# Keys and queries of the first batch in long pieces, turned by products with the identity

## The chip, the core and the metric

The kernel runs on one core of a Trainium2 chip. The metric is device time in microseconds (us) of one launch. The five engines are written as in the profile: PE (TensorE) with PEld (its weight loads), DVE (VectorE), ACT (ScalarE), POOL (GpSimd) and SP (SyncE, which here only issues DMAs). Each engine works through its own list in order and waits at the head of it.

## What is computed

Attention in chunks of 32 tokens, then two MLPs, all in f32:

```
q_c = q[:, :, c_start:c_end]                       # 32 queries
k_ctx, v_ctx = k, v[:, :, c_start-16 : c_end+8]    # cut at the ends of the sequence
scores = q_c @ concat(mem_k, k_ctx).T / 8          # 8 memory keys ahead of 56 others
out[:, :, c_start:c_end] = softmax(scores) @ concat(mem_v, v_ctx)
x = out as 3072 x 512
x = (s * relu(x @ w_in)**2 + b) @ w_out            # 512 -> 2048 -> 512
y = (silu(x @ w_gate) * (x @ w_val)) @ w_out2      # 512 -> 1536 -> 512
```

There are 4 batches of 8 heads, 768 tokens and a head width of 64.

## The kernel before

**Tiles.** Tokens go through attention in 24 groups g of 128 (six per batch, four chunks each), and through the first MLP in 8 blocks t of 384 tokens (three groups). The first MLP has 16 weight columns m of 128: `first_up(t, m)` (U in the lists) makes 12 products into `hp`, DVE and ACT square the result and split it into `ghi` and `glo`, and `first_down(t, m, i)` (D) adds 12 products to the four banks `acc0` to `acc3`. Each weight tile (1 MB, `load_w1`) is split by DVE and ACT into a rounded part and a rest, `w_first`, before it can be used: `split` makes the steps magnitude, bound, shift, sign, rest, hi, lo, of which five to seven are DVE's.

**The first batch.** Groups 0 to 5 (`EARLY`) are prepared in a way of their own. `load_tokens(g)` (K in `LOADS`) fetches keys and queries of one group by four to six DMAs, token by token: each piece of one head and one token is 64 numbers, 256 bytes. `stage_queries` and `stage_keys` turn them with PE's transpose (12 per group) into PSUM, and DVE or ACT copy them to `qt` and `kt`, where every chunk gets its window of 64 keys. Then come, per group, scores (S, `stage_scores`), maximum and shift on DVE, exponential on ACT, the turned probabilities (A, `stage_probs`), the product with the values (V, `stage_values`), normalising on DVE, and the turn into `xhi`, `xlo` (X, `stage_turn`, `stage_x`). Scores and values each take both banks of the pool `ps_a`, so one has to be emptied by DVE before the next may start. The values come through POOL's queue into one of two buffers (`load_values`, `g % 2`).

**Order.** All lists are made ahead by `Plan.run`, a list scheduler with a length for every step and counters for buffers (`rings`, `room`). `START` gives PE's order of the first blocks: the stages of groups 0 to 5 and, among them, five U and four D. `LOADS` chains the first issues on SP's queue; `MOVED` names the steps that go to the other one of DVE and ACT. `LENT` counts the weight slots (of 17) that the first batch borrows.

```
START = (
    "Q0 T0 S0 Q1 T1 A0 V0 Q2 S1 T2 X0 A1 S2 V1 Q3 A2 X1 V2 T3 X2 Q4 S3 U U D T4 D A3 V3 U Q5 "
    "S4 X3 T5 U A4 S5 D V4 A5 X4 V5 D X5 U "
)
```

The last U of `START` is the first of block t = 1; it needs X5. From there on PE has work in an unbroken row of U and D.

Of the kernel before, what the change touches and what calls it, by code (L numbers as in the profile page):

```python
# [10 lines left out]
F32 = mybir.dt.float32  # L11
# [17 lines left out]

START = (  # L30
    "Q0 T0 S0 Q1 T1 A0 V0 Q2 S1 T2 X0 A1 S2 V1 Q3 A2 X1 V2 T3 X2 Q4 S3 U U D T4 D A3 V3 U Q5 "
    "S4 X3 T5 U A4 S5 D V4 A5 X4 V5 D X5 U "
# [12 lines left out]
    "K0 C K1 W0 W1 K2 K3 W3 W7 W2 K4 W5 W8 K5 W4 W6 K6_0 W12 W10 W11 W9 W14 W13 W15 "  # L45
# [102 lines left out]
def attention_and_two_mlps(  # L148
# [53 lines left out]
    LENT = 3  # L202
    EARLY = 2 * GPB

# [10 lines left out]
    ident = const.tile([P, P], F32, name="ident")  # L215
    make_identity(nc, ident)
    sb = const.tile([P, 2], F32, name="sb")
# [78 lines left out]
    def rows(dst, src, b, heads, first, n):  # L296
# [6 lines left out]
    def load_tokens(g):  # L303

        b, gi = divmod(g, GB)
        s0 = gi * GQ
        t = wp.tile([P, 4, H * D], F32, tag="w", name=f"qk{g}")
        tq, ka, kb, sc = (t[:, i] for i in range(4))
        every = slice(0, H)
        a, z = s0 - LEFT, s0 + GQ + RIGHT  # L310
        left, over, n = max(0, -a), max(0, z - S), HALF - NMEM
        rows(ka, mem_k, b, every, 0, NMEM)
        if left:
            rows(ka[NMEM:], k, b, every, 0, left)
        rows(ka[NMEM + left:], k, b, every, a + left, n - left)
        rows(tq, q, b, every, s0, GQ)
        rows(kb, k, b, every, a + n, HALF - over)
        if over:
            rows(kb[HALF - over:], k, b, every, S - over, over)
        loaded.setdefault(g, {}).update(q=tq, ka=ka, kb=kb, sc=sc)  # L320
# [73 lines left out]
    def load_values(g, queue):  # L394
# [3 lines left out]
        n = g % 2  # L398
        if n not in v_bufs:
            v_bufs[n] = ld.tile([P, NC, NP, D + 1], F32, tag=f"v{n}", name=f"v{n}")  # L400
            nc.gpsimd.memset(v_bufs[n][:, :, :, D:], 1.0)
        tv = v_bufs[n]
        for e in range(2):
            p0 = e * KC
            if gi < 2:
                mem = tv[p0:p0 + NMEM]
                queue.dma_start(out=mem[:, 0, :, :D], in_=mem_v[b, e:H:2].rearrange("h s d -> s h d"))
# [1014 lines left out]
```

## Time and profile before

| what | value |
|---|---|
| three runs | 1214.85, 1216.21, 1216.58 us (median 1216.21) |
| the profiled execution: its own time, which is its span | 1216.5 us |
| mean granted TensorE clock | 0.987 of full |
| PE, PEld busy | 1175.4 us (97%), 1116.4 us (92%) |
| DVE, ACT busy | 751.7 us (62%), 502.7 us (41%) |
| POOL busy | 143.6 us (12%) |
| DMA | 175.60 MB, mean 144 GB/s |

A row of the timeline gives the start and the length of a run of equal instructions, its engine and line, what it writes and reads, and in brackets the idle time of its engine before it with what ended that. A table of windows gives each engine's busy time in a stretch; an engine that is idle there waits for another, or has nothing to do.

### The profile page before, as it was taken

The numbers are of one execution on the slowest core, as the hardware profiler recorded it, in microseconds if no ns is written. First come the engines' busy times: TensorE is split into PE (matmuls) and PEld (weight loads), VectorE is DVE, ScalarE is ACT, GpSimd is POOL, SyncE is SP. The second block draws the span as 40 slices with busy tenths as digits, with TensorE's granted clock in tenths as the row PEclk, the third lists the DMA queues.
The fourth block names the chain that finished last, engine by engine and source line by source line (L and its number), as shares of the span: only waits on it lengthen the run. The fifth ranks groups of instructions, "written<-read, shape, count | busy, mean of one in ns | idle before, by whom it ended". The sixth has DMA issues, their size and how long they took to land.

```text
span 1216.5 us, 23342 instructions
## 1 busy us (share of the span) xinstructions
PE 1175.4 (97%) x9220; PEld 1116.4 (92%) x9220; DVE 751.7 (62%) x1324; ACT 502.7 (41%) x865; POOL 143.6 (12%) x232
## 2 busy tenths in 40 slices
PE   5679999999999999999999999999999999999998
PEld 4568999999999999999999999999999999999997
DVE  5789986655555445544487955569853367743343
ACT  3365543233333434332277545446433234432332
POOL 6342013222132223120000000000000000000000
PEclk9689999999999999999999999999999999999999
DMA  9947334222222222220347266386555386465351
GB/s 193 240 115 208 114 94 110 66 45 65 40 53 68 44 66 47 46 55 1 113 182 251 104 235 218 121 318 259 188 229 216 123 331 246 152 247 208 108 204 52
DMA packets 171775, 175.60 MB, mean 144 GB/s; under 512 B 115170, under 2 KB 141090, under 8 KB 170642
## 3 DMA queue, kind: packets, MB, share of 16 engines
q1 hardware_dynamic: 164498, 162.92, 41.7%
q0 software_dynamic: 7168, 11.18, 4.0%
q8 instruction: 73, 1.20, 0.4%
q14 instruction: 36, 0.29, 0.1%
HBM read 125.24 MB, written 48.76 MB: 143 GB/s over the span
## 4 chain that ended last, share of the span: by engine, by line
PE 89%; SPq 7%; DMA 1%; DVE 1%; issue 1%; ACT 0%; DVEq 0%; ACTq 0%
PE acc L615 7%; PE hp L614 7%; PE acc L614 7%; PE acc L616 7%; PE hp L616 7%; PE hp L615 7%; PE chain_A L615 6%; PE chain_A L616 6%; PE oacc L616 6%; PE oacc L615 6%; PE chain_A L614 5%; PE oacc L614 5%; PE chain_B L614 4%; PE chain_B L615 4%; PE chain_B L616 4%; SPq L298 3%
## 5 line engine op out<-in xcount | busy, mean ns | idle before, releaser
L614 PE MATMUL hp<-xhi,w_first 128*128 128x384 f32 x512 | 174.7, 341 | 1.1 <-DVE xhi L232 1.1
L614 PE MATMUL acc<-ghi,w_first 128*128 128x384 f32 x512 | 173.3, 338 | 1.5 <-DVE ghi L667 0.9
L615 PE MATMUL acc<-glo,w_first 128*128 128x384 f32 x512 | 171.9, 336 | 0.9 <-DVE glo L674 0.5
L615 PE MATMUL hp<-xlo,w_first 128*128 128x384 f32 x512 | 172.2, 336 | 0.2 <-DVE xlo L609 0.2
L616 PE MATMUL hp<-xhi,w_first 128*128 128x384 f32 x512 | 172.1, 336 | 0.0
L616 PE MATMUL acc<-ghi,w_first 128*128 128x384 f32 x512 | 171.3, 335 | 0.0
L416 POOL DMA_DIRECT2D v<-in_v_dram x208 | 134.0, 651 | 312.5 <-PE psB L549 266.3
L784 ACT ACTIVATE kept<-chain_A 128x384 f32<-128x384 f32 x144 | 70.8, 492 | 186.0 <-PE chain_A L616 183.9
L615 PE MATMUL chain_A<-ops,hi_up 128*128 128x384 f32 x384 | 130.1, 339 | 0.0
L616 PE MATMUL chain_A<-ops,lo_up 128*128 128x384 f32 x384 | 129.4, 337 | 0.0
L614 PE MATMUL chain_A<-ops,hi_up 128*128 128x384 f32 x384 | 128.4, 334 | 0.0
L654 DVE SCALAR_TENSOR_TENSOR r<-r,sb 128x384 f32<-128x384 f32 x87 | 53.2, 612 | 112.9 <-ACT r L643 112.3
L643 ACT ACTIVATE r<-hp 128x384 f32<-128x384 f32 x98 | 48.0, 490 | 176.1 <-PE hp L616 159.1
L616 PE MATMUL oacc<-w_down,glo 128*128 128x512 f32 x288 | 114.6, 398 | 0.0
L615 PE MATMUL oacc<-w_down,ghi 128*128 128x512 f32 x288 | 113.9, 396 | 0.0
L614 PE MATMUL oacc<-w_down,ghi 128*128 128x512 f32 x288 | 112.1, 389 | 0.0
L614 PEld LDWEIGHTS hp<-xhi,w_first 128*128 128x128 f32 x512 | 96.9, 189 | 2.6 <-issue 1.4
L614 PEld LDWEIGHTS acc<-ghi,w_first 128*128 128x128 f32 x512 | 96.1, 188 | 3.3 <-ACT v L230 1.2
L615 PEld LDWEIGHTS acc<-glo,w_first 128*128 128x128 f32 x512 | 96.1, 188 | 2.7 <-DVE glo L674 1.6
L789 DVE TENSOR_TENSOR kept<-chain_B,kept 128x384 f32<-128x384 f32 x48 | 26.7, 557 | 114.5 <-PE chain_B L616 112.2
L615 PEld LDWEIGHTS hp<-xlo,w_first 128*128 128x128 f32 x512 | 96.9, 189 | 0.5 <-DVE xlo L609 0.5
L616 PEld LDWEIGHTS hp<-xhi,w_first 128*128 128x128 f32 x512 | 96.8, 189 | 0.0
(131 smaller groups left out, 2213.2 us busy)
## 6 DMA issues: line engine op xcount, KB each, us to landing
ops<-ops_dram SPq DMA_DIRECT2D x56, 768.0 KB
ops_dram<-ops SPq DMA_DIRECT2D x28, 768.0 KB
sum_dram<-o SPq DMA_DIRECT2D x48, 256.0 KB
v<-in_v_dram POOLq DMA_DIRECT2D x176, 56.0 KB, 3.4
raw_first<-in_moe_w_in_dram SPq DMA_DIRECT2D x16, 512.0 KB
raw_first<-in_moe_w_out_dram SPq DMA_DIRECT2D x16, 512.0 KB
o<-sum_dram SPq DMA_DIRECT2D x8, 1024.0 KB
y_dram<-y SPq DMA_DIRECT2D x32, 192.0 KB
```

Of the source, the lines that this page charges most:

```text
L298: nc.sync.dma_start(out=dst.rearrange("p (h d) -> p h d", d=D)[:n], in_=src[b, heads, first:first + n, :].rearrange("h s d -> s h d"),)
L416: queue.dma_start(out=tv[r0:r0 + n, c, :, :D], in_=v[b, e:H:2, first:first + n, :].rearrange("h s d -> s h d"),)
L614: nc.tensor.matmul(o, whi, xhi, start=first, stop=False, skip_group_check=onto)
L615: nc.tensor.matmul(o, whi, xlo, start=False, stop=False, skip_group_check=onto)
L616: nc.tensor.matmul(o, wlo, xhi, start=False, stop=last, skip_group_check=onto)
L643: nc.scalar.activation(out=r, in_=hp, func=AF.Relu)
L654: nc.vector.scalar_tensor_tensor(out=r, in0=r, scalar=s_sb, in1=r, op0=ALU.mult, op1=ALU.mult)
L784: nc.scalar.activation(out=t, in_=st2[n]["A"], func=AF.Copy)
L789: nc.vector.tensor_tensor(out=t, in0=st2[n]["B"], in1=kept, op=ALU.add)
```

## The change

Keys and queries of batch 0 no longer come group by group. Two DMAs fetch all keys (four heads each) and four fetch the queries (four heads and half of the partitions each): partition p gets tokens 6p to 6p+5 of a head in one run of 6 x 64 numbers, 1536 bytes. PE turns them for a whole block of 384 tokens at a time: for each pair of heads j and each of the six tokens r of a partition, `turn_pieces` multiplies the pieces (as the stationary side, 64 columns per head) with the identity, and writes the columns into PSUM six apart, which puts the tokens in order. For keys the identity is padded by three columns on either side, so that the window of block u is 69 partitions wide. One copy per pair of heads spreads keys to all twelve chunks of a block (`copy_batch_keys`), into the tiles of `xhi`, `xlo` for block 0 and over the fetched queries for block 1. Six weight slots are borrowed in place of three; values get a third early buffer in one of them. `START`, `LOADS` and `MOVED` are new; groups 1 and 3 (and 6 and 7) now take the exponential head by head on ACT with the maximum as bias, so DVE makes no shift for them. Groups 6 and later are loaded as before.

```diff
-    "Q0 T0 S0 Q1 T1 A0 V0 Q2 S1 T2 X0 A1 S2 V1 Q3 A2 X1 V2 T3 X2 Q4 S3 U U D T4 D A3 V3 U Q5 "
-    "S4 X3 T5 U A4 S5 D V4 A5 X4 V5 D X5 U "
+    "K0 Q0 S0 S2 A0 V0 X0 S1 A1 V1 A2 X1 V2 Q1 X2 K1 U S3 U D A3 S4 U V3 D A4 U X3 S5 D V4 A5 X4 "
+    "D V5 X5 U "
...
-    "K0 C K1 W0 W1 K2 K3 W3 W7 W2 K4 W5 W8 K5 W4 W6 K6_0 W12 W10 W11 W9 W14 W13 W15 "
+    "K6_0 BK0 C BM BK1 BQ00 BQ01 W0 BQ11 W1 BQ10 W2 W3 W6 W5 W4 W8 W7 W9 W12 W11 W10 W14 W13 W15 "
...
-    LENT = 3
     EARLY = 2 * GPB
+    LENT = 6
+    RES = GB * GQ // P
+    PAD = 3
+    EDGE = PAD * RES - LEFT
...
+    def VBUFS(g):
+        return 3 if g < EARLY else 2
...
+    def load_batch(name, src, i, half=None):
+        at = slice(0, P) if half is None else slice(half * (P // 2), (half + 1) * (P // 2))
         nc.sync.dma_start(
-            out=dst.rearrange("p (h d) -> p h d", d=D)[:n],
-            in_=src[b, heads, first:first + n, :].rearrange("h s d -> s h d"),
-        )
+            out=pieces(name)[at].rearrange("p h r d -> p h (r d)"),
+            in_=src[0, 4 * i:4 * i + 4].rearrange("h (p r) d -> p h (r d)", r=RES)[at],
+        )
...
+    def turn_pieces(name, j, ps, rows, turned):
+
+        n = turned.shape[1]
+        to = ps[:, 0:RES * n].rearrange("m (p r) -> m r p", r=RES)
+        for r in range(RES):
+            for e in range(2):
+                nc.tensor.matmul(
+                    to[e * D:(e + 1) * D, r], pieces(name)[rows, 2 * (j % 2) + e, r], turned, start=True, stop=True
+                )
+
+    def stage_batch_keys(u, j):
+        batch["k", u, j] = ps = bank(ps_acc, f"acc{j}", f"psK{u}_{j}")
+        span, first = P // 2 + 2 * PAD - 1, u * P // 2
+        turn_pieces(f"keys{j // 2}", j, ps, slice(0, P), padded[:, first:first + span])
...
+    def copy_batch_keys(engine, u, j):
+        w = batch.pop(("k", u, j))[:, EDGE:EDGE + 1]
+        copy(
+            engine, early_keys(u)[j // 2][:, j % 2, :, NMEM:],
+            bass.AP(tensor=w.tensor, offset=w.offset, ap=[w.ap[0], [CHUNK, GPB * NC], [1, WIN]]),
+        )
...
+    def stage_batch_queries(t, j):
+        pool, tag = (ps_acc, f"acc{j}") if t else ((ps_a, "a"), (ps_h, "h"))[j // 2]
+        batch["q", t, j] = ps = bank(pool, tag, f"psQ{t}_{j}")
+        at = slice(t * (P // 2), (t + 1) * (P // 2))
+        turn_pieces(f"queries{j // 2}", j, ps, at, ident[at, at])
...
-        n = g % 2
+        n = g % VBUFS(g)
```

**SP's queue at the start.** Before, the first ten DMAs (`qk` is a group's tile of keys and queries, `sb_in` two constants):

```order
L298 DMA qk_141<-in_mem_k_dram 8x8x64
L298 DMA qk_141<-in_k_dram 16x8x64
L298 DMA qk_141<-in_k_dram 56x8x64
L298 DMA qk_141<-in_q_dram 128x8x64
L298 DMA qk_141<-in_k_dram 80x8x64
L262 DMA sb_in<-in_moe_s_dram 1x1
L262 DMA sb_in<-in_moe_b_dram 1x1
L298 DMA qk_164<-in_mem_k_dram 8x8x64
L298 DMA qk_164<-in_k_dram 72x8x64
L298 DMA qk_164<-in_q_dram 128x8x64
```

Now, from the fourth DMA on (three small ones for group 6 stand ahead; `keys` and `queries` hold four heads of all 768 tokens, `raw_first` is a weight tile as fetched):

```order
L320 DMA keys_161<-in_k_dram 128x4x384
L270 DMA sb_in<-in_moe_s_dram 1x1
L270 DMA sb_in<-in_moe_b_dram 1x1
L326 DMA keys_161<-in_mem_k_dram 8x8x64
L320 DMA keys_167<-in_k_dram 128x4x384
L320 DMA queries_169<-in_q_dram 64x4x384
L320 DMA queries_207<-in_q_dram 64x4x384
L249 DMA raw_first_226<-in_moe_w_in_dram 128x4x256
L254 DMA raw_first_226<-in_moe_w_out_dram 128x1024
L320 DMA queries_207<-in_q_dram 64x4x384
```

The keys of all six groups and the queries of the first three now come ahead of the first weight tile; before, the keys and queries of two groups did, and those of the other four came between weight tiles.

**PE's list from its first work to the first scores (`psS`).** Before:

```order
L268 MATMUL spread<-ident,sb_in 128x1 x2
L434 MATMUL psQ_175<-ident,qk_141 128x128 x4
L445 MATMUL psK_0_181<-ident,qk_141 128x80 x4
L445 MATMUL psK_1_186<-ident,qk_141 128x80 x4
L481 MATMUL psS_0_213<-kt_205,qt_203 32x64
```

Now (each `psK`, `psQ` row is one turn for a pair of heads):

```order
L276 MATMUL spread<-ident,sb_in 128x1 x2
L377 MATMUL psM<-ident,keys_161 128x8 x4
L336 MATMUL psK_0_180<-ident,keys_161 64x69 x12
L336 MATMUL psK_1_209<-ident,keys_161 64x69 x12
L336 MATMUL psK_2_230<-ident,keys_167 64x69 x12
L336 MATMUL psK_3_245<-ident,keys_167 64x69 x12
L336 MATMUL psQ_0_259<-ident,queries_169 64x64 x12
L336 MATMUL psQ_1_273<-ident,queries_169 64x64 x12
L336 MATMUL psQ_2_288<-ident,queries_207 64x64 x12
L336 MATMUL psQ_3_303<-ident,queries_207 64x64 x12
L537 MATMUL psS_0_332<-early_khi,qt_286 32x64
```

Twelve transposes stood ahead of the first scores; now 96 products do, for three groups at once. The same eight turns for block 1 stand later, just ahead of the first U.

**DVE's list at the last early part of x (`xlo` of group 5).** Before:

```order
L586 TENSOR_TENSOR on_1225<-psV_1_1172,rc_1219 128x4x64
L955 TENSOR_TENSOR w_first_1210<-raw_first_877,w_first_1210 128x1024
L232 CAST xhi_950<-psO_1243 128x4x128
L609 TENSOR_TENSOR xlo_951<-psO_1243,xhi_950 128x4x128
L232 COPY y<-acc_770 128x384
L906 SCALAR_TENSOR_TENSOR raw_first_402<-raw_first_402,t_first_852 128x1024
L913 SCALAR_TENSOR_TENSOR raw_first_402<-raw_first_402 128x1024
```

Now:

```order
L958 TENSOR_SCALAR t_first_1117<-t_first_1117 128x1024
L963 SCALAR_TENSOR_TENSOR raw_first_598<-raw_first_598,t_first_1117 128x1024
L666 TENSOR_TENSOR xlo_1194<-psO_1354,xhi_1193 128x4x128
L1012 TENSOR_TENSOR w_first_1348<-raw_first_663,w_first_1348 128x1024
L970 SCALAR_TENSOR_TENSOR raw_first_598<-raw_first_598 128x1024
L443 STREAM_TRANSPOSE qt_143<-qt_143 128x512
L447 STREAM_TRANSPOSE kin_142<-kin_142 128x640
L451 COPY memT_1398<-kin_142 128x32
L950 TENSOR_SCALAR t_first_1405<-raw_first_1338 128x1024
```

Seven weight tiles were wholly split ahead of this place, and are five now; the sixth and most of the seventh follow it.

## Rows read from the trace of the kernel before

**Rows 1.** The page's 40 slices, 30.4 us each: busy tenths, granted clock, DMA.

```profile
PE   5679999999999999999999999999999999999998
PEclk9689999999999999999999999999999999999999
DMA  9947334222222222220347266386555386465351
```

**Rows 2.** Windows: per engine busy time (x instructions), then granted clock, DMA share, GB/s.

```profile
0.00:12.00 12.00, 4.61 (x81) 3.93 (x82) 2.18 (x6) 1.28 (x1) 9.72 (x23) 1.00 0.92 166
12.00:20.00 8.00, 4.93 (x80) 3.95 (x80) 4.89 (x15) 5.18 (x8) 5.33 (x9) 1.00 1.09 262
20.00:37.00 17.00, 8.33 (x216) 6.53 (x216) 16.42 (x30) 5.07 (x7) 7.21 (x12) 0.87 1.16 231
37.00:52.00 15.00, 7.39 (x152) 5.94 (x152) 7.40 (x15) 5.71 (x10) 9.00 (x13) 0.50 1.07 212
52.00:92.60 40.60, 32.48 (x482) 28.44 (x466) 35.63 (x63) 24.15 (x42) 13.99 (x22) 0.86 0.56 138
92.60:175.30 82.70, 81.35 (x640) 79.36 (x641) 78.54 (x120) 41.84 (x66) 11.77 (x19) 1.00 0.49 139
```

**Rows 3.** Timeline of PE, the front: start, length, what, idle before it.

```profile
8.95 1.27 PE L445 MATMUL psK<-ident,qk 80*128 80x80 f32 x8
10.61 1.34 PE L481 MATMUL psS<-kt,qt 64*32 64x64 f32 x64 [0.38 <-DVE kt L232]
...
24.67 1.09 PE L434 MATMUL psQ<-ident,qk 128*128 128x128 f32 x4 [6.42 <-DMA qk<-in_q_dram]
...
38.23 1.12 PE L534 MATMUL psA<-ident,qk 128*128 128x128 f32 x4 [2.40 <-ACT qk L514]
...
50.09 1.09 PE L434 MATMUL psQ<-ident,qk 128*128 128x128 f32 x4 [6.19 <-DMA qk<-in_q_dram]
51.11 1.19 PE L481 MATMUL psS<-kt,qt 64*32 64x64 f32 x64
52.23 0.69 PE L614 MATMUL hp<-xhi,w_first 128*128 128x384 f32 x1
...
92.59 0.41 PE L614 MATMUL hp<-xhi,w_first 128*128 128x384 f32 x1 [1.08 <-DVE xhi L232]
```

**Rows 4.** The chain of work that ended last, pieces in order of time: start, length, what.

```profile
13.44 6.93 SPq L298
...
37.25 7.45 SPq L298
```

**Rows 5.** DMA queue q1 from 19 to 26 us: packets, MB, share of 16 engines.

```profile
q1 hardware_dynamic: 2820, 0.82, 81.1%
```

**Rows 6.** The same queue from 103 to 115 us, where weight tiles land.

```profile
q1 hardware_dynamic: 4266, 3.86, 104.9%
```

**Rows 7.** Groups by form, DVE, 0 to 100 us: busy us, mean ns, idle before.

```profile
L913 DVE SCALAR_TENSOR_TENSOR raw_first<-raw_first 128x1024 uint32<-128x1024 uint32 x8 | 9.8, 1222 | 0.1
L955 DVE TENSOR_TENSOR w_first<-raw_first,w_first 128x1024 fp32r<-128x1024 f32 x7 | 8.5, 1218 | 0.2 <-ACT w_first L230 0.2
L901 DVE TENSOR_SCALAR t_first<-t_first 128x1024 uint32<-128x1024 uint32 x8 | 5.5, 692 | 0.2
L507 DVE TENSOR_TENSOR qk<-psS,mx 128x256 f32<-128x256 f32 x12 | 4.5, 415 | 0.0
L232 DVE COPY kt<-psK 128x448 f32<-128x448 f32 x4 | 2.5, 615 | 0.0
L232 DVE COPY qt<-psQ 128x512 f32<-128x512 f32 x3 | 2.1, 686 | 0.9 <-PE psQ L434 0.9
L232 DVE COPY kt<-psK 128x64 f32<-128x64 f32 x5 | 1.1, 221 | 4.8 <-ACT kt L230 4.8
```

**Rows 8.** Waits of 0 to 110 us: us in total, times, longest.

```profile
ACT t_first L891 <- DMA raw_first<-in_moe_w_out_dram: 14.1, 3, 7.2
```

**Rows 9.** Timeline of DVE: the last rest of a weight tile's split.

```profile
172.01 1.22 DVE L955 TENSOR_TENSOR w_first<-raw_first,w_first 128x1024 fp32r<-128x1024 f32 x1
```

More of the change, by code (lines that the diff above doesn't have):

```diff
@@ L294, in attention_and_two_mlps, with lent, pieces @@
     v_bufs = {}
-    def rows(dst, src, b, heads, first, n):
+    def VBUFS(g):
+        return 3 if g < EARLY else 2
+    batch = {}
+    def lent(name):
+        if name not in batch:
+            batch[name] = wp.tile([P, 4, 512], F32, tag="w", name=name)
+        return batch[name]
+    def pieces(name):
+        return lent(name)[:, 0:3].rearrange("p a f -> p (a f)").rearrange("p (h r d) -> p h r d", h=4, r=RES)
+    def load_batch(name, src, i, half=None):
+        at = slice(0, P) if half is None else slice(half * (P // 2), (half + 1) * (P // 2))
@@ L997, in plan_queries @@
             return
-        qk = transfer(
-            [], lambda: load_tokens(g), 4, 590, take=["sc"], rate=200.0, name=f"K{g}"
-        )
-        vv = load_v(g)
-        at_[g] = {"v": vv, "qk": qk}
-        t = plan.add(PE, 0.44, lambda: stage_queries(g, early), [qk], take=["acc2"] if early else ["a"])
-        at_[g]["qt"] = either(
-            f"q{g}", {ACT: 0.50, DVE: 0.60}, lambda e: stage_queries_copy(e, g), [t], take=["qt"],
-            give=["acc2"] if early else ["a"],
-        )
@@ new lines, in attention_and_two_mlps, with plan_batch, load @@
+    early_ready = {}
+    def plan_batch():
+        def load(name, src, i, half, of):
+            batch_landed[name] = transfer(
+                [], lambda: load_batch(of, src, i, half), 1, 786 if half is None else 393, rate=BATCH_RATE, name=name
+            )
+        for i in range(2):
+            load(f"BK{i}", k, i, None, f"keys{i}")
+        batch_landed["BM"] = transfer([issues["BK0"]], load_memory, 1, 16, rate=40.0, name="BM")
+        for t in range(2):
+            for i in range(2):
+                load(f"BQ{t}{i}", q, i, t, f"queries{i}")
+        for g in range(VBUFS(0)):
+            at_[g] = {"v": load_v(g)}
@@ new lines, in plan_batch_keys @@
+    def plan_batch_keys(u):
+        done = []
+        if u == 0:
+            t = plan.add(PE, 0.30, stage_memory, [batch_landed["BM"]], take=["h"])
+            batch_landed["m"] = plan.add(DVE, 0.12, copy_memory_keys, [t], give=["h"])
+        for j in range(NP):
+            t = plan.add(
+                PE, 0.78, lambda j=j: stage_batch_keys(u, j), [batch_landed[f"BK{j // 2}"]], take=[f"acc{j}"],
+                put=["w"] * 2 if u and j == NP - 1 else (),
+            )
+            done.append(either(
+                f"k{u}_{j}", {ACT: 0.75, DVE: 0.85}, lambda e, j=j: copy_batch_keys(e, u, j),
+                [t, *(early_ready["q", 1, "pe"] if u else ())],
+                take=["x"] if not u and j == 0 else (), give=[f"acc{j}"],
+            ))
+        for i in range(2):
+            done.append(either(
+                f"m{u}_{i}", {ACT: 0.40, DVE: 0.30}, lambda e, i=i: fill_batch_memory(e, u, i),
+                [batch_landed["m"], *(done[:1] if not u else early_ready["q", 1, "pe"])],
+            ))
+        early_ready["k", u] = done
@@ new lines, in plan_batch_queries @@
+    def plan_batch_queries(t):
+        done, pe = [], []
+        for j in range(NP):
+            ring = [f"acc{j}"] if t else [("a", "h")[j // 2]]
+            p = plan.add(
+                PE, 0.66, lambda j=j: stage_batch_queries(t, j), [batch_landed[f"BQ{t}{j // 2}"]], take=ring,
+            )
+            pe.append(p)
+            done.append(either(
+                f"q{t}_{j}", {ACT: 0.43, DVE: 0.47}, lambda e, j=j: copy_batch_queries(e, t, j), [p],
+                take=() if t else ["r"], give=ring,
+            ))
+        early_ready["q", t], early_ready["q", t, "pe"] = done, pe
```

197 lines of the change are left out of this document (103 added, 94 removed), and 23 rows, old and new, of the table MOVED.

## The prediction

> **What bounds the kernel now.** I read the page's slices first [rows 1]: PE is full from the fourth slice to the end, at full clock. So the time is what PE does from about 92 us on, which the change leaves alone, plus the moment at which that unbroken row begins. Call T0 the start of the fifth U, the first of block t = 1: 92.6 us [rows 3]. The windows say what the front is made of [rows 2]. Up to 52 us the 16 DMA engines are at 0.92 to 1.16 of their time; from 52 to 92.6 us they are at 0.56, and DVE is busy 35.6 of 40.6 us. So two limits follow each other: data until 52 us, then DVE. Added up, DVE works 2.2 + 4.9 + 16.4 + 7.4 + 35.6 = 66.5 us before T0 and idles 26.1.
>
> The timeline of PE shows the data limit twice, 6.4 and 6.2 us of waiting for a group's queries [rows 3]; ACT waits 14.1 us for weight tiles [rows 8], and the chain of waits runs through single token loads that hold SP's queue for 7 us [rows 4]. Between 37 and 52 us DVE is idle for 7.6 of 15 us [rows 2].
>
> The clock: the slices read nearly full in the first one [rows 1], but the row of four transposes at 38.2 us, inside a stretch granted 0.50 [rows 2, 3], lasts 1.12 us, and the like row at 24.7 us lasts 1.09. So I price the front at the lower level, 1.2 GHz, until PE has worked without a gap for some time.
>
> **What the change does, part by part.**
>
> *Loads.* Keys and queries of six groups are 3.46 MB in 256-byte pieces (six groups of 256 KB of queries, 304 KB of keys, 16 KB of memory keys). While such pieces fill the queue it moves 0.82 MB in 81.1% of 7 us, 144 GB/s [rows 5]; a mix of weight tiles and small loads of group 6 moves 3.86 MB in 12.6 us of engine time, 307 GB/s [rows 6]. The change needs 3.16 MB. At 307 that is 10.3 us of the DMA engines instead of 24.0; the ends are 144 (a gain of 2) and 307, and I take 260, 12 us, as 1536-byte pieces are nearer to those of a weight tile. So weight tiles land some 12 us earlier, and the waits for queries at 24.7 and 50.1 us and most of ACT's 14.1 us go. SP's held issues go with them. Two tiles fewer are fetched ahead, so their loads compete later; from 92.6 us on the DMA engines are at 0.49 [rows 2], which hides them, and without that cover one tile costs 1 MB at 307, 3.4 us.
>
> *A later start.* Before, the scores of group 0 ran at 10.6 us. Now all keys and half of the queries, 2.4 MB, with about 0.5 MB of values beside them, must land before the first score, at 166 to 262 GB/s [rows 2] some 12 to 16 us after about 1 us of start-up. PE turns as they land.
>
> *Turns.* Eight turns of twelve products stand ahead of the first score, eight more ahead of the first U. No row has such a product. The 32 score products leave 64 rows in 1.19 to 1.34 us [rows 3]: an f32 product counts twice, a transpose once. The 24 of a turn cost 24 x 0.019 = 0.45 us at the scores' rate. But scores fill eight blocks of the array at a time and a turn two: twelve follow each other in a block instead of eight, each with 69/64 of the columns, and 1.19/8 x 12 x 69/64 = 1.9 us. The far end is one after another at the pace of the 80-column transposes, 24 x 1.27/8 = 3.8 us. I take 1.4, below 1.9 because the scores' 1.19 holds a start and an end that turns in a row pay once, and 0.9 at full clock. First turn at about 8.7 us, when PE's first work before ended too (8.95); eight take 11.2, scores at 20, DVE's first maximum at 21.5 instead of 12.1. **This part costs some 9 us of start.**
>
> A transpose is a mode of its own, and the Trainium skill, "TensorEngine Tiling (Array Packing)", Restrictions, says that column tiling (64 columns here) excludes transpose mode for f32; "TensorE: Matmul & The Clock Gate", Terms, calls that mode four times faster for f32. By it half the batch's queries, three transposes of 1.09 us, would cost 13 us as products, 6.5 in two blocks, 1.6 per turn; the doubled rows agree in kind, and the sum would be 3 us worse.
>
> *DVE's work ahead of T0.* Moved behind T0: one rest (1.22), two lo steps (2.44), five steps of 0.69 (3.46) [rows 7], 7.1 us. Copies of keys and queries: three of 0.686, four of 0.615, five of 0.221 go, 5.6 us; two of 672 columns (0.615 x 1.5) and four smaller, 3.6, come. The shifts of groups 1 and 3 go, 4 x 0.415, for two tiny steps; the rest evens out. Sum 66.5 - 7.1 - 2.0 - 1.4 = 56.0 us.
>
> *DVE's idle time ahead of T0.* 18.9 us until the first maximum (21.5 less 2.6 of early copies). From there to the first U, I walked the list: scores of group 2 wait until DVE has emptied the two banks (1.3), the value product of each group waits for probabilities (about 1 each for three groups), and the eight late turns and the key copies hold the last x of block 0 (about 3): 7. That puts the first U near 50 us (before: 52.2), with 24 of the 56 us of DVE work done and 32 to go; 12% of waiting, as in 35.6 of 40.6 before, adds 4.5. Sum 30.4, so **T0 = 56.0 + 30.4 = 86.4 us**, 6.2 earlier.
>
> *Other parts.* The third buffer lets the values of group 2 be fetched at once, not after those of group 0 are used. PE's long waits in the front are for queries [rows 3], so I price it at nothing; POOL, busy 7.2 of 17 us from 20 us on [rows 2], covers the issues. The head-by-head exponential puts eight ACT steps of 64 columns in place of one; at the 0.22 of DVE's 64-column copies [rows 7] that is 1.8 us per group. ACT was busy 24.2 of 40.6 us there [rows 2], which hides it; if not, it costs 3.5.
>
> *After T0.* DVE is busy 78.5 of 82.7 us from T0 to the 20th further U [rows 2], and the last weight tile is ready at 173.2 for a use at 175.3 [rows 9, 2]. It has nothing to give. But what the change moves behind T0 (7.1) is nearly offset by what groups 6 and 7 lose there (two shifts and a sum each) and by casts that now are ACT's: counted by the same prices, DVE has 0.7 us less from T0 to the last tile than before. New there is that the eighth and ninth weight loads stand on SP's queue behind four stores of block 0, which wait for D number four; they are issued near T0, and DVE reaches the first some 4 us later. I price this at nothing; if DVE stands there, `glo` behind it stands too, and PE loses up to 3.
>
> **Sum.** 1216.5 - 6.2 = 1210.3 us in terms of the profiled execution, whose span stands 0.3 over the median. I predict **1210.4 us**. A measurement of this kernel tells 0.2%, 2.4 us, from no change.
>
> **The rivals.**
>
> 1. *Quicker turns.* PE warms within the first eight turns, which come without a gap (before, PE worked 4.6 of the first 12 us [rows 2]), and waits are fewer than I walked. Turns at 0.9 take 4 off the start and as much off the second eight, of which DVE passes on about half: T0 79 to 83, 1203 to 1207. Against it: DVE's in-order list. Chance 0.20.
> 2. *The front leaks as before.* The data limit goes but DVE waits a fifth of the time behind the first U, 8 us in place of 4.5, and up to 2 more ahead of it, because more steps hang on one another. T0 90 to 92, 1214 to 1216. For it: at 37 to 52 us DVE idled half the time [rows 2], surely not all for data. With it goes the case that the gain is given back behind T0. Chance 0.11.
> 3. *Products instead of transposes.* Each turn takes about 1.7 at the lower level, by the doubled rows; 16 x 0.3 = 4.8 later: 1215. Chance 0.08. The rule of the Trainium skill's "TensorEngine Tiling (Array Packing)" above is this case.
> 4. *Slower: turns one after another.* If two blocks don't run beside each other, or writing columns six apart slows PSUM, a turn takes 2.8, half of the transposes' far end and more. Then scores start at 31 us and the late eight add 6: T0 100 to 104, 1224 to 1228. It decides against the change from 1.8 us per turn on, where 16 x 0.4 eats the 6.2. Against it: the scores' rows, which can't reach 1.19 us one after another. Chance 0.15.
> 5. *It does nothing* is no case of its own: the lists do change as described; 1216 is the edge of rival 2.
>
> **Numbers.** The forecast has 0.46 (1207.5 to 1213.8), rival 1 0.20, so faster by over 0.2% is 0.66; rivals 2 and 3 make no difference, 0.19; rival 4 is 0.15. The range 1204 to 1220 leaves out the lower tail of rival 1 (about 0.05) and most of rival 4 (0.13).
>
> **What would show it.** Right: first score at 18 to 21 us, no wait of PE for queries behind it, a turn row of about 1.4 us, DVE idle 28 to 33 us before T0, T0 at 84 to 89, PE full from there. Wrong: a turn row over 1.8, a first score past 25, an idle of ACT for weight tiles, gaps of PE behind T0 for `glo` or `w_first`.

## The result, and the profile after

The changed kernel takes 1224.16 us (median of five runs, 1220.46 to 1224.77) against 1216.21 (1213.53 to 1217.27) before: ratio 1.0062, 95% interval 1.0039 to 1.0085. A second measurement gave 1224.05 against 1214.54, 1.0078 (1.0061 to 1.0096). It is slower by 0.6 to 0.8%; 1210.4 was predicted.

The profiled execution spans 1222.4 us, 5.9 more than the one before. This difference is too small: for 32 other executions of the kernel before the span is on record, 1210.8 to 1216.4 us with a median of 1212.8, so that the profiled one (1216.5) is longer than all of them, while 1222.4 is usual for the changed kernel (median 1222.3 in the second measurement). Some 4 of the 8.0 to 9.5 us that were lost can't be found by comparing the two profiles; where the kernel before is usually quicker than in its profile isn't known. The slices of the changed kernel answer to [rows 1]:

```profile
PEclk9999999999999999999999999999999999999999
DMA  9927335222223222220347275296565386465251
```

The clock record of this execution begins only at about 60 us, so the first two nines of PEclk say nothing. That the front ran at the lower level can be seen further down, in a second execution.

PE's timeline answers to [rows 3]; a row gives start, length, what, and the wait ahead of it:

```profile
8.30 3.03 PE L336 MATMUL psK<-ident,keys 128*64 128x69 f32 x48
13.83 3.03 PE L336 MATMUL psK<-ident,keys 128*64 128x69 f32 x48 [2.49 <-DMA keys<-in_k_dram]
16.78 5.39 PE L336 MATMUL psQ<-ident,queries 64*64 64x64 f32 x96
22.10 0.68 PE L537 MATMUL psS<-early_khi,qt 64*32 64x64 f32 x32
...
28.28 0.67 PE L606 MATMUL psV<-v,at 64*32 64x65 f32 x14 [0.69 <-ACT at L238]
30.91 1.07 PE L606 MATMUL psV<-v,at 64*32 64x65 f32 x50 [1.96 <-issue]
...
38.62 1.37 PE L591 MATMUL psA<-ident,queries 128*128 128x128 f32 x4 [3.07 <-ACT queries L581]
...
44.50 1.17 PE L606 MATMUL psV<-values,at 64*32 64x65 f32 x59
49.39 0.43 PE L606 MATMUL psV<-values,at 64*32 64x65 f32 x5 [3.72 <-issue]
49.75 5.38 PE L336 MATMUL psQ<-ident,queries 64*64 64x64 f32 x96
55.06 1.13 PE L650 MATMUL psO<-ident,on 128*128 128x128 f32 x4
56.12 5.09 PE L336 MATMUL psK<-ident,keys 128*64 128x69 f32 x96
61.15 0.45 PE L671 MATMUL hp<-xhi,w_first 128*128 128x384 f32 x1
```

The waits for queries of [rows 3] are gone. A turn costs what was predicted: four query turns in 5.39 us, 1.35 each. But the first U comes at 61.2 us, not near 50 as forecast (52.2 before): the second eight turns, and the turn of the last x between them, stand in one closed row of 11.4 us ahead of it. Ahead of that PE stops inside two value products, for no releaser that the profile knows ("issue").

DVE's busy time, in windows cut at the first maximum, the first U and T0 (columns as in [rows 2]):

```profile
0.00:23.60 23.60, 13.83 (x264) 13.14 (x264) 2.43 (x8) 6.08 (x11) 14.45 (x30) 1.00 0.93 205
23.60:61.15 37.55, 24.27 (x537) 20.14 (x537) 24.39 (x48) 18.88 (x39) 23.40 (x37) 1.00 1.07 231
61.15:93.06 31.91, 26.11 (x508) 23.73 (x504) 29.48 (x56) 24.77 (x50) 15.34 (x23) 1.00 0.31 67
```

T0 is 93.06, against 92.59 before and 86.4 predicted. DVE works 2.4 + 24.4 + 29.5 = 56.3 us ahead of it, and idles 21.2, 13.2 and 2.4. Before, in stretches cut at the same three events, it worked 66.5 us and idled 9.9, 11.4 and 4.7. So the change did take 10.2 us of work from DVE ahead of T0, and gave it 10.7 us more of waiting, more than all of that ahead of the first maximum (11.3).

Rows of DVE in the middle stretch: its waits at two value products and at the late turns, and two rows without a wait that are used further down (the normalising of group 2 and the end of the last x of block 0):

```profile
32.00 0.23 DVE L628 TENSOR_SCALAR rc<-psV 128x4 f32<-128x4 f32 x2 [2.69 <-PE psV L606]
...
49.86 0.23 DVE L628 TENSOR_SCALAR rc<-psV 128x4 f32<-128x4 f32 x2 [4.08 <-PE psV L606]
...
50.36 0.75 DVE L643 TENSOR_TENSOR on<-psV,rc 128x256 f32<-128x256 f32 x2
...
53.90 0.56 DVE L240 COPY turned<-psQ 128x384 f32<-128x384 f32 x1 [1.59 <-PE psQ L336]
55.18 0.56 DVE L240 COPY turned<-psQ 128x384 f32<-128x384 f32 x1 [0.72 <-PE psQ L336]
56.23 0.69 DVE L240 CAST xhi<-psO 128x512 fp32r<-128x512 f32 x1 [0.49 <-PE psO L650]
56.95 0.69 DVE L666 TENSOR_TENSOR xlo<-psO,xhi 128x512 fp32r<-128x512 f32 x1
```

From T0 to the end it is 1222.4 - 93.1 = 1129.3 us, and was 1216.5 - 92.6 = 1123.9. Nearly all of these 5.4 us are lost at two places. The first is T0 itself; the timeline of PE there:

```profile
93.06 0.45 PE L671 MATMUL hp<-xhi,w_first 128*128 128x384 f32 x1 [0.69 <-ACT xhi L238]
94.26 0.54 PE L672 MATMUL hp<-xlo,w_first 128*128 128x384 f32 x1 [0.76 <-DVE xlo L666]
...
97.48 0.52 PE L673 MATMUL hp<-xhi,w_first 128*128 128x384 f32 x1
```

Behind waits of 2.1, 0.7 and 0.8 us between 89.6 and 94.3 us the granted clock is 0.5 (1.2 GHz) from 94.5 to 97.9 us, and a product takes 0.52 us in place of 0.33; the first U of block 1 needs 4.7 us where it needed 2.7. The second place is at 249 us (DVE, then PE):

```profile
243.67 0.71 DVE L443 STREAM_TRANSPOSE qt<-qt 128x512 f32<-128x512 f32 x1 [4.44 <-DMA kin<-in_k_dram]
```

```profile
249.09 0.44 PE L671 MATMUL acc<-ghi,w_first 128*128 128x384 f32 x1 [2.41 <-DVE ghi L724]
```

DVE stands at the turn of group 11's queries and keys, whose pieces SP goes on issuing until 240 us (until 233.6 before). `ghi` and `glo` are behind it in the list, and one U comes 7.7 us after the one ahead of it where 4.5 was the rule: 3.2 us.

### The profile page after: what moved, and what is told of

Same layout as the page of the kernel before. It is cut to its first block, busy times and chain, and to the rows that moved or that the text cites. A ratio compares the mean times of both kernels' runs of the same rounds, so it can differ in the third digit from the quotient of the medians.

```text
span 1222.4 us, 24007 instructions
## 1 busy us (share of the span) xinstructions
PE 1185.3 (97%) x9536; PEld 1127.1 (92%) x9536; DVE 739.0 (60%) x1301; ACT 518.9 (42%) x930; POOL 145.0 (12%) x235
## 4 chain that ended last, share of the span: by engine, by line
PE 87%; DMA 6%; DVE 3%; issue 1%; ACT 1%; SPq 1%; POOL 0%; DVEq 0%; POOLq 0%; ACTq 0%
PE hp L671 6%; PE acc L672 6%; PE acc L671 6%; PE hp L673 6%; PE acc L673 6%; PE hp L672 6%; PE chain_A L672 6%; PE chain_A L673 6%; PE oacc L673 6%; PE oacc L672 5%; PE chain_A L671 5%; PE oacc L671 5%; PE chain_B L671 4%; PE chain_B L673 4%; PE chain_B L672 4%; DMA raw_first<-in_moe_w_out_dram 2%
## 5 line engine op out<-in xcount | busy, mean ns | idle before, releaser
L491 POOL DMA_DIRECT2D v<-in_v_dram x190 | 121.9, 648 | 300.9 <-PE psB L606 277.5
L711 DVE SCALAR_TENSOR_TENSOR r<-r,ident 128x384 f32<-128x384 f32 x92 | 56.3, 612 | 113.8 <-ACT r L700 111.2
L700 ACT ACTIVATE r<-hp 128x384 f32<-128x384 f32 x103 | 50.6, 491 | 175.1 <-PE hp L673 163.3
L671 PE MATMUL chain_B<-ops,hi_up 128*128 128x384 f32 x288 | 96.4, 335 | 0.0
```

The source lines that it names most:

```text
L491: queue.dma_start(out=tv[r0:r0 + n, c, :, :D], in_=v[b, e:H:2, first:first + n, :].rearrange("h s d -> s h d"),)
L671: nc.tensor.matmul(o, whi, xhi, start=first, stop=False, skip_group_check=onto)
L700: nc.scalar.activation(out=r, in_=hp, func=AF.Relu)
L711: nc.vector.scalar_tensor_tensor(out=r, in0=r, scalar=s_sb, in1=r, op0=ALU.mult, op1=ALU.mult)
```

## The experiments

My first theory was that the front is still bound by its loads: the chain of waits of the changed kernel starts with four value loads.

```profile
3.65 7.68 DMA v<-in_v_dram
11.62 8.07 DMA v<-in_v_dram
19.97 8.23 DMA v<-in_v_dram
28.48 7.59 DMA values<-in_mem_v_dram
```

Rivals: the new lists as such, the turns, and a separate loss at 249 us. A time below is the median of a run's executions. T0 and first U are those of its one profile, and that execution can stand above the median: by 3.0 to 4.1 us for the pieces of 256 bytes, every turn twice, the spread turns and the turns of 128 columns. Four profiles with the same lists of PE and DVE ahead of T0 (the changed kernel twice, the held weights, the queries through POOL) give T0 at 93.1, 95.6, 92.5 and 92.4 and the first U at 61.2, 62.2, 60.2 and 60.5; so a shift under 3 us says nothing.

### Values on SP's queue

```diff
-    "K6_0 BK0 C BM BK1 BQ00 BQ01 W0 BQ11 W1 BQ10 W2 W3 ...
+    "K6_0 BK0 C BM BK1 V0 BQ00 BQ01 V1 W0 BQ11 V2 BQ10 W1 W2 W3 ...
```

> Loads theory (up to 52 us the DMA engines are full, and the values of groups 0 to 2, which come through POOL's queue, land too late; the chain of waits of the changed kernel runs through four of their loads from 3.7 to 36.1 us): with these values on SP's queue, between keys and queries and ahead of W0, the memory copies of group 2's values end by 28 us instead of 36.6, the first U comes at 53 to 58 us instead of 61.2, T0 at 87 to 91 instead of 93.3, the time 1217 to 1221 if the stall of 3.2 us at 249 us stays. Lists theory (the new order of the lists loses the time, whatever the loads do): first U within 1.5 us of 61.2, T0 92 to 95, time 1222 to 1226. Against both: the 34 issues hold SP for some 17 us, W0 lands after 30 us instead of 19.6, and DVE stands without a tile to split: T0 95 or later, slower than 1226.

1222.69 us (1221.13 to 1225.07). First U 57.7, as the loads theory said, but T0 94.7: the stretch from the first U to T0 grew to 37.0 us. Earlier values are worth about 3.5 us at the first U and nothing at T0. It is no clean test: the issues of the values put the first weight tile's load at 20.9 us in place of 5.3, and DVE is left with 32.3 us of work between first U and T0 in place of 29.5.

### Weight tiles held back

```diff
+HELD = ("first2", "first3", "first6", "first5", "first4")
...
-        raw = wp.tile([P, 2, 2 * 512], U32, tag="w", name=f"raw_{name}")
+        raw = wp.tile([P, 2, 2 * 512], U32, tag="w", name=f"raw_{name}"); name in HELD and nc.gpsimd.memset(raw[:, 0, 0:1], 0)
```

> Weight tiles W2, W3 and W6 may be fetched only when POOL has issued the values of group 3, W5 after those of group 4, W4 after those of group 5 (a one-column memset on their tile stands in POOL's list). Loads theory: the same values through the same queue now share the DMA engines with fewer packets from about 25 us on; those of group 2 land 3 to 6 us earlier, PE's waits of 2.0 and 3.7 us inside the value products (28 to 50 us) shrink to under 1 each, first U at 54 to 58 us, T0 88 to 92, time 1217 to 1222. Lists theory: first U 60 to 62, T0 92 to 95, 1222 to 1226. If DVE needs the held tiles: first U earlier but T0 later than 94, slower than 1226.

1223.48 us (1220.19 to 1225.24), first U 60.2, T0 92.5. The DMA engines were indeed relieved (a window of this run; DMA share and GB/s last; 1.07 and 237 in the changed kernel in the same 11 us):

```profile
28.00:39.00 11.00, 4.03 (x133) 2.93 (x132) 7.00 (x16) 5.58 (x11) 7.46 (x12) 0.50 0.59 113
```

Nothing came of it, and PE stopped inside the same value products for 3.1 and 2.0 us (and 2.2 us in the first scores). The loads theory falls for this part: the front is full of transfers, and they don't set its end.

### Pieces of 256 bytes again

The layout of `pieces` changes with this, token by token with the four heads side by side.

```diff
-        nc.sync.dma_start(
-            out=pieces(name)[at].rearrange("p h r d -> p h (r d)"),
-            in_=src[0, 4 * i:4 * i + 4].rearrange("h (p r) d -> p h (r d)", r=RES)[at],
-        )
+        for h in range(4):
+            nc.sync.dma_start(
+                out=pieces(name)[at, h], in_=src[0, 4 * i + h].rearrange("(p r) d -> p r d", r=RES)[at])
```

> Keys and queries of the first batch land in pieces of 256 bytes again (per partition token by token, the four heads of a token side by side; 24 DMAs in place of 6), all else as in the changed kernel. If long pieces are what the change lives on: 3.16 MB take some 21 us of the DMA engines in place of 14.4 (144 GB/s as in [rows 5]), the first scores start at 25 to 30 us instead of 22.1, first U 64 to 69, T0 96 to 101, time 1227 to 1232. If the loads stand beside other work (holding three weight tiles back until 40 us moved the first U by 1 us only): first scores 22 to 24, first U 61 to 63, T0 93 to 95, time 1222 to 1226.

1226.78 us (1225.73 to 1229.8), T0 97.9: 2 to 5.5 us later at T0, 2.6 in the time. The long pieces bring something, between the two cases; it is less than half of the 12 us of DMA time that I had saved.

### Every turn twice

```diff
-            for e in range(2):
+            for e in (0, 1, 0, 1):
```

> Every product of the sixteen turns is issued twice (the second writes the same columns again), 1.35 us more per turn, 10.8 us more ahead of the first scores and 10.8 more ahead of the first U. Loads theory: the first four turns stand between loads and cost 3 of their 5.4 us, the others all of theirs, first U 75 to 80 us; DVE, which then splits weights in the time it has, passes about half on: T0 99 to 106, time 1230 to 1237. Turns theory (the price of a turn is what decides against the change): T0 later by all 21 us, 112 to 116, time 1242 to 1247. If PE in the front is hidden behind loads and DVE: T0 93 to 96, 1224 to 1228.

1236.56 us (1232.95 to 1239.61), first U 76.3, T0 108.5. Extra turns of 16 x 1.35 = 21.6 us move T0 by 13 to 16 us and the time by 12.4. From the first U to T0 it stays 32.3 us (31.9 in the changed kernel):

```profile
76.25:108.53 32.28, 26.45 (x509) 23.89 (x505) 28.35 (x54) 24.61 (x49) 14.82 (x22) 0.97 0.19 54
```

DVE had 15 us more ahead of the first U, but did only 1.5 us more of its work there (28.4 for 26.8), since the other splits stand behind steps of attention in its list. So it is again left with 28.4 us of work between first U and T0, and is idle for only 3.9 us there.

### One row of turns twice

```diff
-            for e in range(2):
+            for e in (0, 1, 0, 1)[:4 if block == 0 else 2]:
```

and `block == 1` in the second kernel (`block` is handed in by the callers).

> Only the eight turns of block 0, ahead of the first scores, issue every product twice: 10.8 us more of PE, of which the wait for keys at 13 us hides 2 to 3. By the prediction's own model (the start is passed on in full): T0 8 to 11 us later than 93 to 96, that is 101 to 107. If the loads set the start: T0 93 to 98. Added to the other run's shift it should come to the 15.5 us of all sixteen doubled, within 4.

> Only the eight turns of block 1, in the row just ahead of the first U, issue every product twice: 8 to 10.8 us more of PE. By the prediction's model (about 3 of their 11 us are on the path, DVE goes on splitting weights beside them): T0 96 to 99. By the chain theory (block 1's scores hang on these turns, and T0 follows the first U by 32 us whatever DVE did before): first U 69 to 73, T0 101 to 106.

The first eight doubled: 1225.89 us (1223.01 to 1228.76), T0 97.7, 2 to 5 us later. The second eight doubled: 1234.41 us (1229.49 to 1236.8), first U 70.6, T0 102.9, 7 to 10.5 us later. PE's timeline, first kernel, then second:

```profile
20.31 6.90 PE L336 MATMUL psQ<-ident,queries 64*64 64x64 f32 x128 [2.77 <-issue]
29.16 2.61 PE L336 MATMUL psQ<-ident,queries 64*64 64x64 f32 x42 [1.95 <-issue]
...
38.04 0.35 PE L537 MATMUL psS<-early_khi,qt 64*32 64x64 f32 x6 [2.47 <-issue]
...
55.49 1.96 PE L336 MATMUL psQ<-ident,queries 64*64 64x64 f32 x58
58.94 1.32 PE L336 MATMUL psQ<-ident,queries 64*64 64x64 f32 x38 [1.49 <-issue]
...
60.87 3.10 PE L336 MATMUL psK<-ident,keys 128*64 128x69 f32 x96
63.90 0.45 PE L671 MATMUL hp<-xhi,w_first 128*128 128x384 f32 x1
```

```profile
50.81 10.85 PE L336 MATMUL psQ<-ident,queries 64*64 64x64 f32 x192
...
62.65 8.03 PE L336 MATMUL psK<-ident,keys 128*64 128x69 f32 x192
70.60 0.44 PE L671 MATMUL hp<-xhi,w_first 128*128 128x384 f32 x1
```

The late turns, then, weigh more than I had assumed. The second kernel is the clean case: it has the stops of the changed kernel, at the same products, and 8.4 more us in the row are 8.4 to 10.4 more at the first U and 7 to 10.5 at T0. The first kernel changed more than one thing. Its scores came 9.6 us later, 4.7 of it by two new stops among the doubled products. Behind that the two stops inside value products (5.7 us) were gone, others of 2.5 and 1.5 us had come, the clock stood at full level from 55 us on, and the second eight turns took 6.4 us in place of 10.5. So its small shift doesn't show that the first eight turns are cheap. In the times the two rows add 1.8 and 10.3 us, together 12.1, and all sixteen add 12.4.

### Turns of 128 columns

In the layout with 256-byte pieces two heads lie side by side.

```diff
-            for e in range(2):
-                nc.tensor.matmul(
-                    to[e * D:(e + 1) * D, r], pieces(name)[rows, 2 * (j % 2) + e, r], turned, start=True, stop=True
+                nc.tensor.matmul(
+                    to[:, r], pieces(name)[rows, 2 * (j % 2):2 * (j % 2) + 2, r].rearrange("p h d -> p (h d)"), turned, ...
```

> Loads as in the run with 256-byte pieces; in this layout two heads lie side by side, so that a turn is six products of 128 columns in place of twelve of 64. To be read against that run. Turns theory (turning by products is what eats the gain: issuing them twice moved T0 by 15.5 us for 21.6 us of PE): if a product of 128 columns takes as long as one of 64, a turn falls from 1.35 to 0.7 us, T0 comes 6 to 9 us earlier than in that run. If two of 64 columns ran beside each other already, a turn stays at 1.2 to 1.35 us; PE has 192 instructions fewer ahead of the first U, so at most one wait of 2 to 4 us for instructions less: T0 0 to 3 us earlier. If PE's front is no limit, T0 within 1 us of that run.

1234.94 us (1234.08 to 1239.07), T0 108.4, 10.5 later than with twelve products: a turn takes 2.63 us, twice as long, which none of the three cases held.

```profile
11.55 10.51 PE L335 MATMUL psK<-ident,keys 128*128 128x69 f32 x48
21.99 10.50 PE L335 MATMUL psQ<-ident,queries 64*128 64x64 f32 x48
```

A pair of products of 64 columns takes 0.22 us, and one of 128 takes 0.44. That the two of a pair run beside each other fits these rows, but isn't shown by them. The f32 transposes of [rows 3] need 1.09 / 4 = 0.27 us for 128 columns of moving data, these products 10.50 / 24 = 0.44 for 64: 3.2 times as much per column. The Trainium skill, "TensorE: Matmul & The Clock Gate", Terms, calls transpose mode four times faster for f32; that agrees in kind.

### The program's own pieces

```diff
-        for j in range(NP):
+        for j in [*range(NP)] * 12:
             nc.tensor.transpose(
                 ps[:, j * NMEM:(j + 1) * NMEM], ...
```

> The four small transposes of the memory keys are issued twelve times over, at 8 us, where PE waits 2.5 us for keys soon after: 44 products with 44 weight loads more ahead of everything else on PE. PE stops inside the value products of groups 0 and 2 (after 14 of 64, 2.0 us, and after 59 of 64, 3.7 us) just when a 16 KB piece of its program is being fetched. Program theory: the stops move forward by those 88 instructions, out of the value product of group 0 into the scores of group 2 and to the first third of the value product of group 2. Data theory (PE waits for values): the stops stay where they are. Either way first scores up to 3 us later and the time within 4 us of the changed kernel's.

1229.94 us (one run), 5.8 to 5.9 above the changed kernel's medians and so outside the 4 that were expected; T0 98.1. The stops moved, and there are five ahead of the first U where there were two, of 1.3, 3.9, 3.4, 3.1 and 0.7 us:

```profile
26.01 0.50 PE L537 MATMUL psS<-early_klo,qt 64*32 64x64 f32 x7
30.45 0.65 PE L537 MATMUL psS<-early_klo,qt 64*32 64x64 f32 x24 [3.93 <-issue]
31.02 1.12 PE L591 MATMUL psA<-ident,queries 128*128 128x128 f32 x4
32.83 1.38 PE L606 MATMUL psV<-v,at 64*32 64x65 f32 x64 [0.69 <-ACT at L238]
...
49.85 0.49 PE L606 MATMUL psV<-values,at 64*32 64x65 f32 x15
53.40 0.98 PE L606 MATMUL psV<-values,at 64*32 64x65 f32 x49 [3.06 <-issue]
```

Group 2's value product now stops after 15 of 64, 44 products sooner, as many as were put in; that of group 0 runs through, and the stop stands 24 + 4 + 14 = 42 products sooner, in the scores. So PE waits there for its program, not for data. In the changed kernel the DMA view of 45.5 to 49.5 us shows the piece (queue, packets, MB, share):

```profile
q8 instruction: 1, 0.02, 2.1%
```

The whole run has 75 such pieces for PE's 9536 products and as many weight loads, 254 instructions a piece. Narrower windows of the same view tell when a piece is moved: at 27.7 and 46.4 us in the changed kernel, whose stops end at 30.9 and 49.4, and at 50.8 us here, where the last row above starts at 53.4. So in these three PE goes on 2.6 to 3.2 us after the piece is moved; the move itself takes about 0.1 us. The kernel before had one such stop ahead of T0, behind its first U:

```profile
72.44 0.46 PE L481 MATMUL psS<-kt,qt 64*32 64x64 f32 x11 [2.57 <-issue]
```

### Order and lists of the front

Exponentials of groups 1 and 3 in one piece (both out of `MOVED`):

```diff
-    "a10 a12 a5 a7 a9 e1 e3 e6 e7 g0_0 ...
+    "a10 a12 a5 a7 a9 e6 e7 g0_0 ...
```

> Groups 1 and 3 take one exponential of 512 columns behind DVE's shift, as before the change, in place of eight of 64 on ACT. PE-chain theory (first U is set by PE's waits and turns in a row; one is 3.1 us for ACT's exponentials of group 1): this wait falls under 1.5 us, the first U comes 1 to 3 us earlier (58 to 60), T0 91 to 93, time 1221 to 1224. DVE theory (T0 is DVE's work and its idle time): DVE gets 4 shifts of 0.4 and two sums more, 2 to 3 us: T0 94 to 96, time 1225 to 1228.

1224.07 us (1220.86 to 1227.6), first U 61.3, T0 95.1. PE's wait for group 1's exponential shrank from 3.1 to 2.2 us only; a stop of the program beside it grew. No difference.

The second eight turns spread over PE's waits:

```diff
-    "K0 Q0 S0 S2 A0 V0 X0 S1 A1 V1 A2 X1 V2 Q1 X2 K1 U ...
+    "K0 Q0 S0 S2 A0 V0 Q1 X0 S1 A1 V1 K1 A2 X1 V2 X2 U ...
```

> The eight turns for block 1 no longer stand in one row ahead of the first U: the query turns stand behind the value product of group 0, the key turns behind that of group 1, where PE waits 13 us in all for DVE, ACT and values. PE-chain theory: 4 to 8 us of those 10.5 fall into waits, first U 54 to 58, T0 87 to 91, time 1216 to 1221. DVE theory: first U earlier, but DVE's work stays, T0 92 to 95, time 1222 to 1226. If the queries for block 1 land after 31 us, PE waits for them in the middle: first U 62 or later, T0 95 or later.

1224.94 us (1221.96 to 1228.58), first U 65.3, T0 101.0: the third case. PE waits 2.3 us for queries and every step of block 0 is late by the turns ahead of it, which fill no wait, since each wait ends on a chain through ACT and DVE that starts later too. T0 is later for another reason as well: the planner now puts seven whole splits of weight tiles ahead of it in place of five, and DVE works 65.0 us ahead of T0 in place of 56.3. The profiled execution is the slowest of four, 3.6 us over the median; from T0 on it takes 1125.8 us, without the wait at 249. The median is only 0.8 us above the changed kernel's.

The planner told of PE's slowness:

```diff
-            n=len(self.tasks), engine=engine, length=length, ...
+            n=len(self.tasks), engine=engine, length=length * (self.slow if engine == "PE" else 1.0), ...
...
-        what, g = item[0], int(item[1:] or 0)
+        what, g = item[0], int(item[1:] or 0); plan.slow = 1.0 if ups else 1.9
```

> Same instructions, other lists: the planner counts PE's steps ahead of the first U as 1.9 times as long (it had 0.66 and 0.78 us for a turn that takes 1.35 to 1.5, 0.44 for four transposes that take 1.1). DVE then gets the splits of four weight tiles ahead of the first U where it had two. Lists theory (the front's DVE stands in order behind PE steps that the planner thought would be done, idle 31 of 52 us, and T0 is the first U plus the splits that are left): DVE's work ahead of the first U rises from 27 to 32 us or more, T0 falls to 84 to 90, time 1214 to 1220. PE-chain theory (T0 follows PE's row of turns, scores and products, whatever DVE does beside it): first U 60 to 63, T0 92 to 95, time 1222 to 1226. If splits now stand ahead of attention steps before their tile has landed: first U after 64, slower than 1226.

> The last kernel and, with it, the queries of groups 9 to 11 through POOL's queue. If the wait at 249 us is in the other's lists as well, this one is 2 to 3 us faster than it; if the new lists no longer have it, they are the same within 1 us. With the lists theory this is the version that could beat both kernels: 1211 to 1217.

1233.85 us (1231.33 to 1234.83) and, with the queries through POOL, 1232.87 (1230.97 to 1237.13); T0 107.0 and 104.8. The last case: DVE now stands at the first weight tile's magnitude ahead of group 0's maximum, and PE's value product waits behind that (DVE, then PE):

```profile
26.54 0.69 DVE L954 TENSOR_SCALAR t_first<-t_first 128x1024 f32<-128x1024 f32 x1 [7.24 <-ACT t_first L948]
```

```profile
39.28 1.02 PE L606 MATMUL psV<-v,at 64*32 64x65 f32 x33 [7.17 <-ACT at L238]
```

Four tiles were split at 62.5 us, where the changed kernel had two, but T0 came 11 to 15 us later. DVE's window up to T0 says why:

```profile
0.00:106.97 106.97, 65.13 (x1304) 57.36 (x1304) 73.96 (x131) 55.83 (x105) 52.27 (x89) 0.76 0.78 182
```

The new lists put nine whole splits ahead of T0 in place of five. DVE works 74.0 us there in place of 56.3 and idles 33.0 in place of 36.8, so T0 is later by the added work. The run therefore doesn't test what was meant, the same work done earlier.

### Behind T0

```diff
-            nc.sync.dma_start(
+            (nc.gpsimd if 9 <= g <= 11 else nc.sync).dma_start(
                 out=qin[:, j], in_=q[b, h, s0:s0 + GQ, ds]...
```

> Queries of groups 9 to 11 are fetched through POOL's queue instead of SP's, which is busy without a break from 172 to 260 us. Late theory (3.2 of the lost us arise at 249 us, where DVE stands 4.4 us for the last key and query pieces of group 11, which SP issues until 240): that wait is under 1 us, the U that began at 252.4 begins at 248.5 to 250, T0 stays at 93 to 94, time 1219 to 1222. Rival (that wait stands in for another that ends at the same time): the same U begins within 1 us of 252.4 and the time stays at 1223 to 1225.

> The changed kernel once more, unaltered, to be compared on one chip with the two kernels of other lists below. By every theory 1220 to 1225 us; the wait of 3.2 us at 249 us may be there in some runs and not in others, which would spread them over some 3 us.

Queries of groups 9 to 11 through POOL: 1221.98 us (1220.79 to 1224.73), T0 92.4, no wait of DVE at 238.7 (the turn follows its predecessor at once), and the U that had come 7.7 us after the one ahead comes after 4.5. The changed kernel again: 1224.05 us (1222.45 to 1228.34); there T0 is 95.6 and that U comes after 5.0, so the wait takes up what the front varies by. From T0 to the end it is 1127.5 us through POOL and 1126.7 in this second profile of the changed kernel, against 1129.3 in the first. So the wait at 249 us is gone, but a gain in the time isn't shown: against the kernel before, the ratio is 1.0061 through POOL, and 1.0062 and 1.0078 for the changed kernel.

The second profile of the changed kernel has the clock of the front (windows; granted clock third from the right):

```profile
23.60:62.20 38.60, 23.07 (x547) 18.78 (x537) 24.32 (x48) 18.88 (x39) 24.07 (x38) 0.58 1.07 229
```

None of these versions beats the kernel before.

## Why the prediction was wrong

**Right.** The turn of 1.35 us for 1.4. (By the rule in the Trainium skill, "TensorE: Matmul & The Clock Gate", Terms, the estimate had been 1.6.) DVE's work ahead of T0, 56.3 for 56.0. That the waits for queries go. DVE's stretch behind the first U: it was busy for 29.5 of 31.9 us there, forecast 32 of 36.5. Full work of PE from T0 on, but for the two places above. The start was nearly right, a first maximum at 23.6 for 21.5, with the first score at 22.1 for 18 to 21.

**The step that failed** is DVE's idle time between the first maximum and the first U: "scores of group 2 wait until DVE has emptied the two banks (1.3), the value product of each group waits for probabilities (about 1 each for three groups), and the eight late turns and the key copies hold the last x of block 0 (about 3): 7. That puts the first U near 50 us". It was 13.2 us, and the first U came at 61.2. DVE's rows show where. The banks cost 1.3, and the late turns with the last x 1.59 + 0.72 + 0.49 = 2.8, as forecast. The rest, 9 us in place of 3, stands at probabilities and value products, and 2.69 + 4.08 of it behind the two products in which PE stopped for its program for 1.96 and 3.72 us. For these stops the sum had no term. The rest of the sum: 2.3 too little until the first maximum, 2.1 too much after the first U. Together 56.3 + 21.2 + 13.2 + 2.4 = 93.1.

**The late turns.** On the way to the first U they weigh more than DVE's idle time tells. I let a quarter of their 11 us pass. By the rows of PE and DVE about 7.5 of the 10.5 us hold the first U: the turn of the last x could have begun at 51.1 us, when DVE had normalised group 2, in place of 55.1, and that x was complete at 57.6 us, 3.5 ahead of the first U (an estimate from one trace). Doubling the row showed that each further us there is an us at the first U. DVE used part of this time for splits, 26.8 us of work ahead of the first U in place of 24, and had that much less to do after it. No run takes out the stops or the turns, so how the lost time divides between them stays open.

**The model behind it.** T0 is DVE's work plus DVE's idle time in every run, and the split of the two tells which runs compare. In the runs with doubled turns the work ahead of T0 stays at 56 to 57 us and only the waiting grows, because DVE follows its list in order and can't draw later splits into an earlier wait. In the runs with other lists the work itself moved ahead of T0.

**Loads.** The 12 us of DMA time were taken as 12 us of earlier weight tiles. Holding tiles back until 40 us cost nothing, and short pieces cost 2 to 5.5 us at T0, so that was about the worth of the long ones in this order of loads. It is paid back by the turns: by [rows 3] six groups took 6 x (1.09 + 1.27) = 14.2 us of transposes, sixteen turns take 21.6, and these 7.4 us at the 0.60 to 0.75 of the doubling are 4.4 to 5.5. That this sum closes is my reckoning; a kernel with these loads and transposes was not tried.

**After T0** I allowed nothing, up to 3 for `glo` behind a weight tile. 5.4 were lost: 2.1 at T0 by waits and the lower clock, and 3.2 at 249 us, with `glo` behind group 11's pieces. That the second hangs on SP's queue is shown by the run through POOL; the second profile of the changed kernel nearly lacks it (0.4 us), with the same median. Why SP's queue runs 5 to 7 us later there is only partly seen: it starts group 9's pieces 2.9 us later than before, about as far as PE is behind by then, and stores in its list wait 2.1 us for their data. The clock's part at T0 was read, not tried.

**The base.** The sum took a span of 1216.5 us as 0.3 over the median of the times. On record a time of the kernel before stands 2.0 to 2.2 us over the span of its execution, so this execution answers to about 1218.6, 2.4 over the median. The table ahead of the prediction, which calls the span the execution's own time, has the same slip.

**Rivals.** Rival 4 gave the time, 1224 to 1228, by luck: its turns of 2.8 us and its T0 of 100 to 104 did not come. Its point that the turns weigh heavily on T0 did, with 0.60 to 0.75 for all sixteen. Rival 2 (the front leaks, the gain is given back behind T0) is what the profile looks like, at T0 92 to 96 and 3 to 5 us lost later; I had it end at 1216.

## What to carry to other kernels

Before pricing work as hidden, find what the next step really waits for: most of PE's row of turns was on the path because the whole next block hung on it. Doubling each suspect on its own, at two places, is a cheap way to learn that; leaving it at one doubled run would have named the turns but not which. But look at what else the doubling moved: more instructions shift the places at which PE stops for its program, and a planner that is told other lengths also moves work across the mark that you measure to. A chain of waits names the last releaser, not the price: its four value loads could go and T0 stayed. And place the execution that was profiled among the others before comparing two profiles; here the comparison hid some 4 us of a loss of 8 to 9.5.

## What was not expected of the hardware

**Program pieces stop PE.** Where PE runs short products (some 0.02 to 0.06 us each with its weight load), it uses up a piece of some 254 instructions in a few us and can then wait up to 4 us for the next 16 KB, at a moving place in the program. The Trainium skill, "Runtime: NRT & Kernel Launch", Instruction fetch mechanics, gives the same 16 KB, with 256 instructions, and calls the cost of a border mostly hidden; here it was 1.96 and 3.72 us in one profile, and 0.7 to 3.9 at five places in that with moved borders, so the measurement decides. Less traffic did not cure it: with weight tiles held back the first of these stops took 3.1 us while the DMA engines were at 0.59.

**Wider is not faster.** A product with 128 stationary columns took four times the time of one half of a pair with 64 (0.44 against 0.11 us).

**More work made later work faster.** With the first eight turns doubled the clock was granted in full from 55 us on, after PE had worked from 51.5 us without a wait; in the changed kernel the stop of 3.72 us cuts this row. The same second eight turns then took 6.4 us in place of 10.5.
